# Gated linear attention plus a squared-ReLU MLP: later units' loads moved to GpSimd's queue, the K~ᵀv product one head pair behind, and three smaller moves

## The chip, the cores and the metric

The kernel runs on one core of a Trainium2 chip. The metric is the device time of one execution in microseconds (us); less is better. It was run three times for timing, and once more under the hardware profiler.

## The reference

A linear-attention recurrence with a complex decay runs over 768 steps for 4 batches and 8 heads of width 48. Its output, as 3072 rows of 384 numbers, goes through an MLP with a squared ReLU.

```python
mag = np.sqrt(a_re * a_re + a_im * a_im)
scale = np.minimum(mag, 0.999) / (mag + 1e-06)
a_re_n, a_im_n = (a_re * scale, a_im * scale)
for t in range(S):                      # S = 768
    ...
    S_re = ar * S_re - ai * S_im + kv   # kv = k_t outer v_t, per head
    S_im = ar * S_im + ai * S_re_old
    y[:, :, t] = einsum('bhd,bhde->bhe', q[:, :, t], S_re)
x = y.transpose(0, 2, 1, 3).reshape(3072, 384)
h = x @ w_in                            # 384 -> 2048
out = (np.maximum(h, 0) ** 2) @ w_out   # 2048 -> 384
```

## The kernel before

The work is cut into 8 **units**: a batch and one half (384 steps) of its sequence. A unit goes through four lists of small closures.

- **chain** (`chain_work`): `load` fetches a, q, k and v of the unit; VectorE (DVE) and ScalarE (ACT) normalise the decays (`roots`, `normalise`, `inverse`); `totals` turns totals per step group with TensorE (PE; tile `tot`) and `scan` multiplies them up on DVE; `back` turns them back (`bk`, copied to `xn`), and `apply` makes the decayed q and k (tile `QK`). The eight heads are two halves, z = 0 and z = 1: a, q, k, the `QK` tiles and the roots come in two parts. At its end `apply` writes k to a DRAM scratch (`rows<-QK`) and reads it back with time on the partitions (`KC<-rows`), both as DMAs of GpSimd's (POOL's) queue.
- **pair** (`pair_work`): for each of four head pairs, `turn` transposes q and k by step group c = 0, 1, 2 (PE `tq`, then ACT copies to `QKT`); `score` makes the causal scores (PE `sa`, DVE masks them into `A`); `keep` makes K~ᵀv (PE `kv`) and the running state (`St`, `S`); `mix` multiplies both out into `ypair`, ACT copies that to `yt`, and DMAs of SyncE's (SP's) queue put its rows into `xT`, the MLP's input.
- **hidden**: 16 blocks of 128 hidden columns (PE `h`, three matmuls each, one per 128 rows of `xT`); ACT squares into `g`. **project**: 3 row blocks in four parts of four matmuls (PE `o`), then `ot` to the output through SP's queue.

`merge` interleaves lists by relative position. In the steady part each merge holds hidden and project of unit n, pair of unit n+1 and chain of unit n+2. Before it come unit 0's chain; unit 0's pair list merged with the conversion of w_in; unit 1's chain and unit 0's hidden; unit 1's pair list merged with the conversion of w_out; unit 2's chain. The inputs are float64, and `convert` makes float32 of 32 weight pieces: one ACT instruction for the lower words (`more`), three on DVE. The merged program is then reordered within each engine by a scheduler with costs of its own, so the order in which an engine runs is not that of the code. Each engine works its own list in order.

Tiles that an engine waits for: `a` and `qk` have one buffer per half, so a load waits until `apply` of the unit before has written `QK`. The PSUM pools are `trp` (2 buffers, for `tq`, `kv`, `tot`, `bk`), `scp` (2, `sa`), `yp` (1, `ypair`) and `dp` (3, `h` and `o`).

Of the kernel before, what the change touches and what calls it, by code (L numbers as in the profile page):

```python
# [481 lines left out]
def fast_path(ctx, tc, q, k, v, a_re, a_im, moe_w_in, moe_w_out, out, flag):  # L482
# [26 lines left out]
    dve, pool, act = nc.vector, nc.gpsimd, nc.scalar  # L509
# [7 lines left out]
    wst = ctx.enter_context(tc.tile_pool(name="wst", bufs=4))  # L517
    trp = ctx.enter_context(tc.tile_pool(name="trp", bufs=2, space=PSUM))
# [3 lines left out]
    dp = ctx.enter_context(tc.tile_pool(name="dp", bufs=3, space=PSUM))  # L522
# [31 lines left out]
    wide = moe_w_in.dtype != F32  # L554
# [12 lines left out]
    raws = {}  # L567

    def fetch(i):
# [10 lines left out]
            out=raw.rearrange("p (m f) two -> p m (f two)", m=src.shape[1]), in_=src)  # L580
        after(get, mark["landed"])

    def convert(i):

        if wide:
            dst, _ = piece(i)
            raw = raws[i]
            lo, hi = raw[:, :, 0], raw[:, :, 1]
            bits = dst.bitcast(U32)

            more = wst.tile([C, DM], U32, name="more", tag="more", bufs=2)
            act.activation(out=more, in_=lo, func=AF.Copy, scale=2.0 ** -29)
# [7 lines left out]
            dve.tensor_tensor(out=bits, in0=bits, in1=more, op=ALU.add)  # L600
        n = i + (NF // 2 if i < NF else 4)
        if n < (NF if i < NF else 2 * NF):
            fetch(n)
# [19 lines left out]
    def load(u):  # L623
        def src(ap):
            return ap[u["b"], :, ts(u["half"], L), :]

        for name, pair in (("a", (a_re, a_im)), ("qk", (q, k))):
            for z in range(2):
                t = u[name, z] = nat.tile([C, 2, HH, W, D], F32, name=f"{name}{z}",
                                          tag=f"{name}{z}")  # L630
                for j, ap in enumerate(pair):
                    nc.sync.dma_start(
                        out=t[:, j].rearrange("p h c d -> p h (c d)"),
                        in_=src(ap)[ts(z, HH)].rearrange(LOADS, c=W))
        if u["n"] == 0:

            gate = const.tile([C, 2], F32, name="gate")
            pool.tensor_copy(out=gate[:, 0:1], in_=u["a", 0][:, 1, HH - 1, W - 1, D - 1:D])
            mark["landed"] = pool.tensor_copy(out=gate[:, 1:2],
                                              in_=u["a", 1][:, 1, HH - 1, W - 1, D - 1:D])  # L640
        u["v"] = pr.tile([C, NM, H, D], F32, name="v", tag="v")
        for j in range(W):
            nc.sync.dma_start(out=u["v"][:, j],
                              in_=src(v).rearrange("h (j s) d -> s j h d", s=C)[:, j])

    def flat(t):
        return t.rearrange("p h c d -> p (h c d)")
# [211 lines left out]
                            in_=rows.rearrange("(j p) e -> p j e", p=C)[:, 0:n])  # L859


    def turn(u, i, c):

        if c == 0:
            u.setdefault("T", {})[i] = pr.tile([R, 4, L], F32, name="QKT", tag="QKT")
        z = 2 * i // HH
        ps = trp.tile([R, 4, C], F32, name="tq", tag="tr")
        for j in range(2):
            for h in range(2):
                hh = (2 * i + h) % HH  # L870
                src = u["K", z][:, c, hh] if j else u["Q", z][:, hh, c]
                nc.tensor.transpose(ps[:, 2 * j + h], src, ident)  # L872
        act.copy(out=u["T"][i].rearrange("r z (p c) -> r c z p", c=W)[:, c], in_=ps)  # L873

    def score(u, i, h):

        T = u["T"][i]
        if h == 0:
            u.setdefault("A", {})[i] = pr.tile([C, 2, NM, C], F32, name="A", tag="A")
        sa = scp.tile([C, NM, C], F32, name="sa", tag="sc")  # L880
        for j in range(NM):
            nc.tensor.matmul(sa[:, j], lhsT=T[:, 2 + h, ts(j, C)], rhs=T[:, h, ts(j, C)],  # L882
                             start=True, stop=True)
        dve.tensor_tensor(out=u["A"][i][:, h], in0=sa, in1=mask3, op=ALU.mult)  # L884
# [3 lines left out]
    def keep(u, i):  # L888

        late = u["half"] > 0  # L890
        n = NM - u["half"]
        if i == 0 and not late:
            state[u["b"]] = wk.tile([R, H, D], F32, name="S", tag="S", bufs=2)
        total_s = state[u["b"]][:, 2 * i:2 * i + 2]
        ps = trp.tile([R, NM, 2, D], F32, name="kv", tag="tr")
        for j in range(n):
            for h in range(2):
                hh = 2 * i + h
                nc.tensor.matmul(ps[:, j, h], lhsT=u["KC", hh // HH][:, j, hh % HH],  # L899
                                 rhs=u["v"][:, j, hh], start=True, stop=True)  # L900
        st = pr.tile([R, 2, 2, D], F32, name="St", tag="St")
        u.setdefault("S", {})[i] = [total_s if late else None, st[:, 0], st[:, 1]]
        outs = [st[:, 0], st[:, 1], total_s]
        before = total_s if late else None
        for j in range(n):
            if before is None:
                act.copy(out=outs[j], in_=ps[:, j])
            else:
                dve.tensor_tensor(out=outs[j], in0=ps[:, j], in1=before, op=ALU.add)
            before = outs[j]  # L910
# [26 lines left out]
    def pair_work(u):  # L937
        w = []
        for i in range(NP):
            w += [[lambda i=i: turn(u, i, 0)], [lambda i=i: turn(u, i, 1)],  # L940
                  [lambda i=i: turn(u, i, 2)]]
# [163 lines left out]
```

## Time and profile before

| | us |
|---|---|
| median of 3 timed runs (841.29 to 846.20) | 844.82 |
| the profiled execution | 853.49 |
| its span, from first to last instruction | 851.8 |
| PE busy in the span (86%) | 728.8 |
| DVE busy (61%) | 519.6 |
| ACT busy (48%) | 407.5 |
| POOL busy (8%) | 65.5 |
| chain that ended last: PE's share | 46% |
| the same: DVE, DMA | 18%, 10% |

The page gives busy time by engine, the span in 40 slices with the granted PE clock, the chain of work that ended last, and the costliest groups of instructions with what their engine waited for. Times in the views are from the span's start. A float32 matmul is one row in the program's order and two halves in the trace. Unit 0's `QK` is ready at 56 us, unit 1's at 157, unit 2's at 247, unit 3's at 314; then a merge ends at 404, 497, 591 and 687, where the next unit's `QK` is ready and its pair list begins. I call those places **boundaries**.

### The profile page before, as it was taken

The page shows a single profiled execution, that of the slowest core. Times are in us where ns is not written, and L with a number is a line of the kernel's source. Part 1 is how long each engine was busy: PE and PEld are TensorE (multiplying, and loading weights), DVE is VectorE, ACT ScalarE, POOL GpSimd, SP SyncE. Part 2 cuts the span into 40 slices and gives each one's busy share as a digit, 9 for nine tenths or more (in the row PEclk, how much of TensorE's full clock was granted, in tenths as well). Part 3 has the DMA queues.
Part 4 walks back from the last instruction along what each step waited for, and adds up shares of the span by engine and source line. Part 5 has one row for each costly group of instructions (what it writes and reads, how often), then busy time and mean ns, then how long its engine had stood idle before and what let it go on. Part 6 is the DMA issues. An engine that isn't in the chain of part 4 may idle for free.

```text
span 851.8 us, 9873 instructions
## 1 busy us (share of the span) xinstructions
PE 728.8 (86%) x3474; PEld 471.4 (55%) x3474; DVE 519.6 (61%) x1316; ACT 407.5 (48%) x769; POOL 65.5 (8%) x107
## 2 busy tenths in 40 slices
PE   0138978499999989999699988999699989999995
PEld 0026644376556656666466655666466656666552
DVE  5895669978996985658472866378463856500000
ACT  5524377354657608931495237811693225411500
POOL 4003000120000000000000010000000034200000
PEclk9995779689999999999899998999899999999998
DMA  9337110662033026000800062002700178500000
GB/s 289 99 124 226 44 33 1 203 219 71 18 111 120 24 74 183 8 17 17 266 7 8 18 212 45 8 17 71 213 7 8 34 248 271 188 17 26 1 9 23
DMA packets 77114, 76.23 MB, mean 89 GB/s; under 512 B 29184, under 2 KB 68224, under 8 KB 77056
## 3 DMA queue, kind: packets, MB, share of 16 engines
q0 software_dynamic: 10496, 42.47, 14.8%
q1 hardware_dynamic: 66560, 33.04, 14.2%
q8 instruction: 29, 0.48, 0.2%
q14 instruction: 29, 0.24, 0.1%
HBM read 56.62 MB, written 14.16 MB: 83 GB/s over the span
## 4 chain that ended last, share of the span: by engine, by line
PE 46%; DVE 18%; DMA 10%; issue 3%; ACT 3%; SPq 1%; POOL 0%; POOLq 0%; ACTq 0%
PE h L953 20%; PE o L967 14%; DVE fa L786 5%; PE sa L882 3%; PE tq L872 3%; DMA a<-in_a_im_dram 3%; DMA xT<-yt 2%; PE ypair L918 2%; DMA look<-in_moe_w_in_dram 2%; PE kv L899 2%; PE ypair L923 2%; DMA look<-in_moe_w_out_dram 2%; DVE QK L849 1%; DMA KC<-rows 1%; DVE fb L789 1%
## 5 line engine op out<-in xcount | busy, mean ns | idle before, releaser
L953 PE MATMUL h<-xT,w 128*128 128x384 f32 x768 | 284.3, 510 | 27.1 <-DMA xT<-yt 23.9
L967 PE MATMUL o<-w,g 128*128 128x384 f32 x768 | 266.0, 492 | 0.0
L953 PEld LDWEIGHTS h<-xT,w 128*128 128x128 f32 x768 | 142.7, 199 | 110.3 <-issue 33.4
L967 PEld LDWEIGHTS o<-w,g 128*128 128x128 f32 x768 | 140.8, 192 | 83.5 <-issue 3.7
L873 ACT COPY QKT<-tq 96x512 f32<-96x512 f32 x96 | 80.8, 845 | 59.0 <-PE tq L872 58.8
L958 ACT ACTIVATE g<-h 128x384 f32<-128x384 f32 x128 | 62.0, 487 | 84.1 <-PE h L953 83.7
L872 PE MATMUL tq<-ident,QK 128*96 128x128 f32 x384 | 66.2, 304 | 24.9 <-DVE QK L849 14.5
L872 PEld LDWEIGHTS tq<-ident,QK 128*96 128x96 f32 x384 | 48.3, 141 | 55.3 <-issue 28.1
L959 ACT ACTIVATE g<-g 128x384 f32<-128x384 f32 x128 | 66.3, 523 | 2.4
L882 PEld LDWEIGHTS sa<-QKT 96*128 96x128 f32 x384 | 55.1, 207 | 17.0 <-ACT QKT L873 4.6
L882 PE MATMUL sa<-QKT 96*128 96x128 f32 x384 | 58.3, 295 | 2.6 <-ACT QKT L873 2.6
L884 DVE TENSOR_TENSOR A<-sa,mask 128x384 f32<-128x384 f32 x64 | 35.0, 553 | 41.4 <-PE sa L882 40.9
L971 ACT COPY ot<-o 128x384 f32<-128x384 f32 x24 | 11.4, 476 | 99.9 <-PE o L967 99.8
L786 DVE TENSOR_TENSOR fa<-e 128x192 f32<-128x192 f32 (+1 forms) x56 | 23.9, 455 | 55.7 <-ACT e L759 55.1
L856 POOL DMA_DIRECT2D rows<-QK x16 | 9.2, 574 | 479.5 <-DVE QK L849 312.6
L849 DVE TENSOR_TENSOR QK<-qk,a 128x576 f32<-128x576 f32 x64 | 44.6, 750 | 0.0
L899 PEld LDWEIGHTS kv<-v,KC 128*96 128x96 f32 x320 | 35.4, 183 | 12.8 <-issue 8.7
L918 PE MATMUL ypair<-A,v 128*48 128x128 f32 x384 | 42.1, 292 | 0.0
L1048 DVE TENSOR_SCALAR flag<-cnt 1x1 int32<-1x1 f32 x1 | 0.1, 145 | 68.4 <-PE cnt L1047 68.4
L899 PE MATMUL kv<-v,KC 128*96 128x48 f32 x320 | 35.2, 262 | 5.3 <-issue 2.7
L757 PE MATMUL tot<-ident,last 128*128 128x128 f32 x72 | 13.8, 295 | 28.8 <-ACT last L719 25.4
L657 ACT ACTIVATE fa<-a 128x1152 f32<-128x1152 f32 x16 | 18.6, 1160 | 39.5 <-DMA a<-in_a_im_dram 39.5
(104 smaller groups left out, 854.0 us busy)
## 6 DMA issues: line engine op xcount, KB each, us to landing
rows<-QK POOLq DMA_DIRECT2D x16, 576.0 KB, 4.7
raw<-in_moe_w_in_dram POOLq DMA_DIRECT2D x16, 384.0 KB, 6.5
raw<-in_moe_w_out_dram POOLq DMA_DIRECT2D x16, 384.0 KB, 4.4
look<-in_moe_w_in_dram POOLq DMA_DIRECT2D x16, 384.0 KB, 4.8
look<-in_moe_w_out_dram POOLq DMA_DIRECT2D x16, 384.0 KB, 4.2
a<-in_a_re_dram SPq DMA_DIRECT2D x16, 288.0 KB, 4.2
a<-in_a_im_dram SPq DMA_DIRECT2D x16, 288.0 KB, 4.9
qk<-in_q_dram SPq DMA_DIRECT2D x16, 288.0 KB, 5.4
```

The costliest lines, as they stand in the source:

```text
L786: dve.tensor_tensor(out=t, in0=x, in1=y[:, j].unsqueeze(1).to_broadcast(shape), op=ALU.mult)
L849: done = dve.tensor_tensor(out=o[:, :, :, r * D:(r + 1) * D], in0=qk[:, j], in1=a[:, r], op=ALU.mult)
L872: nc.tensor.transpose(ps[:, 2 * j + h], src, ident)
L873: act.copy(out=u["T"][i].rearrange("r z (p c) -> r c z p", c=W)[:, c], in_=ps)
L882: nc.tensor.matmul(sa[:, j], lhsT=T[:, 2 + h, ts(j, C)], rhs=T[:, h, ts(j, C)], start=True, stop=True)
L884: dve.tensor_tensor(out=u["A"][i][:, h], in0=sa, in1=mask3, op=ALU.mult)
L899: nc.tensor.matmul(ps[:, j, h], lhsT=u["KC", hh // HH][:, j, hh % HH], rhs=u["v"][:, j, hh], start=True, stop=True)
L918: nc.tensor.matmul(ypair[64 * h:64 * h + D, ts(j, C)], lhsT=u["v"][:, j, 2 * i + h], rhs=A[:, h, j], start=True, stop=S_j is None)
L953: nc.tensor.matmul(ps, lhsT=w1[:, f, m], rhs=u["xT"][:, m], start=(m == 0), stop=(m == NM - 1))
L958: act.activation(out=t, in_=ps, func=AF.Relu)
L959: act.activation(out=t, in_=t, func=AF.Square)
L967: nc.tensor.matmul(u["o"], lhsT=u["g"][f][:, ts(c, C)], rhs=w2[:, f], start=(f == 0), stop=(f == NF - 1))
```

## The change

- Loads of units 2 to 7 are issued by POOL's queue, not SP's. SP keeps the loads of units 0 and 1, the `xT` rows and the output.
- `keep(i)` follows pair i+1's turns and precedes its scores, and `mix(i)` stands between those two scores; three empty slots at the list's end bring the last `mix` forward.
- In units 0 and 1 the `tq` of group c = 1 and `kv` take their PSUM buffer from `dp`, not `trp`.
- The first state of a batch is copied from PSUM by DVE, not ACT.
- The lower words of a weight piece are taken by ACT one piece ahead.
- Two empty slots follow `load` in the chain list.

```diff
+    def lower(i):
+        if wide:
+            more = mores[i] = wst.tile([C, DM], U32, name="more", tag="more", bufs=2)
+            act.activation(out=more, in_=raws[i][:, :, 0], func=AF.Copy, scale=2.0 ** -29)
     def convert(i):
+        if i % NF == 0:
+            lower(i)
...
-            act.activation(out=more, in_=lo, func=AF.Copy, scale=2.0 ** -29)
...
+        if (i + 1) % NF:
+            lower(i + 1)
...
+        get = nc.sync if u["n"] < 2 else nc.gpsimd
...
-                    nc.sync.dma_start(
+                    get.dma_start(
                         out=t[:, j].rearrange("p h c d -> p h (c d)"),
...
-            nc.sync.dma_start(out=u["v"][:, j],
+            get.dma_start(out=u["v"][:, j],
...
+    def bank(u, shape, name, more):
+        pool, tag = (dp, "d") if more and u["n"] < 2 else (trp, "tr")
+        return pool.tile(shape, F32, name=name, tag=tag)
...
-        ps = trp.tile([R, 4, C], F32, name="tq", tag="tr")
+        ps = bank(u, [R, 4, C], "tq", c == 1)
...
-        ps = trp.tile([R, NM, 2, D], F32, name="kv", tag="tr")
+        ps = bank(u, [R, NM, 2, D], "kv", True)
...
-                act.copy(out=outs[j], in_=ps[:, j])
+                dve.tensor_copy(out=outs[j], in_=ps[:, j])
...
             if i:
-                w.append([lambda i=i: mix(u, i - 1)])
-            w += [[lambda i=i, h=h: score(u, i, h)] for h in range(2)]
-            w.append([lambda i=i: keep(u, i)])
-        w += [[], [lambda: mix(u, NP - 1)]]
+                w += [[lambda i=i: keep(u, i - 1)], [lambda i=i: score(u, i, 0)],
+                      [lambda i=i: mix(u, i - 1)], [lambda i=i: score(u, i, 1)]]
+            else:
+                w += [[lambda h=h: score(u, 0, h)] for h in range(2)]
+        w += [[lambda: keep(u, NP - 1)], [], [lambda: mix(u, NP - 1)], [], []]
...
-        return ([lambda: load(u)] + both(roots, normalise, inner, measure_roots, inverse)
+        return ([lambda: load(u), lambda: None, lambda: None] + both(roots, normalise, inner, measure_roots, inverse)
```

**The queues at the boundary at 404 us.** SP before: the eight loads of unit 5 (a, then q and k, for each half), an output store (`out_dram`), and the last two row transfers of unit 4 (`xT`) behind all of them.

```order
L973 DMA out_dram<-ot 128x384
L632 DMA a_2848<-in_a_re_dram 128x4x144
L632 DMA a_2848<-in_a_im_dram 128x4x144
L632 DMA qk_2854<-in_q_dram 128x4x144
L632 DMA qk_2854<-in_k_dram 128x4x144
L632 DMA a_2851<-in_a_re_dram 128x4x144
L632 DMA a_2851<-in_a_im_dram 128x4x144
L973 DMA out_dram<-ot 128x384
L632 DMA qk_2857<-in_q_dram 128x4x144
L632 DMA qk_2857<-in_k_dram 128x4x144
L934 DMA xT<-yt 48x384 x2
L643 DMA v<-in_v_dram 128x8x48 x3
```

POOL after, at the same place; before, only the two `rows` and then the two `KC` stood here.

```order
L866 DMA rows<-QK 128x1152
L642 DMA a_2848<-in_a_re_dram 128x4x144
L642 DMA a_2848<-in_a_im_dram 128x4x144
L642 DMA qk_2854<-in_q_dram 128x4x144
L868 DMA KC<-rows 128x3x384
L866 DMA rows<-QK 128x1152
L642 DMA a_2851<-in_a_re_dram 128x4x144
L642 DMA a_2851<-in_a_im_dram 128x4x144
L642 DMA qk_2854<-in_k_dram 128x4x144
L868 DMA KC<-rows 128x3x384
L642 DMA qk_2857<-in_q_dram 128x4x144
L642 DMA qk_2857<-in_k_dram 128x4x144
```

The loads have left SP's list; on POOL's, the second half's loads now stand behind the first `KC`, which waits until its `rows` have landed.

**PE and ACT at the same boundary.** PE before, from unit 3's last projections over unit 4's last `mix` (six `ypair` rows) to its first `h`:

```order
L967 MATMUL o<-w_109,g 128x384 x8
L918 MATMUL ypair<-A,v 48x128 x2
L923 MATMUL ypair<-QKT,S 48x128 x2
L918 MATMUL ypair<-A,v 48x128 x2
L923 MATMUL ypair<-QKT,St 48x128 x2
L918 MATMUL ypair<-A,v 48x128 x2
L923 MATMUL ypair<-QKT,St 48x128 x2
L872 MATMUL tq<-ident,QK 96x128 x4
L953 MATMUL h<-xT,w_108 128x384 x2
L872 MATMUL tq<-ident,QK 96x128 x4
L953 MATMUL h<-xT,w_108 128x384 x2
```

PE after:

```order
L933 MATMUL ypair<-A,v 48x128 x2
L938 MATMUL ypair<-QKT,S 48x128 x2
L933 MATMUL ypair<-A,v 48x128 x2
L938 MATMUL ypair<-QKT,St 48x128 x2
L933 MATMUL ypair<-A,v 48x128 x2
L938 MATMUL ypair<-QKT,St 48x128 x2
L982 MATMUL o<-w_109,g 128x384 x8
L887 MATMUL tq<-ident,QK 96x128 x4
L968 MATMUL h<-xT,w_108 128x384 x3
L887 MATMUL tq<-ident,QK 96x128 x4
L968 MATMUL h<-xT,w_108 128x384 x3
```

The eight `o` have moved between the last `mix` and the first `h`. ACT before, from the first half's `a` of unit 5 (its square, L657, the first of `roots`) to the first `QKT`:

```order
L657 ACTIVATE fa_2876,sums<-a_2848 128x1152
L971 COPY ot<-o 128x384
L662 ACTIVATE fa_2876<-fb_2877 128x576
L663 ACTIVATE fa_2876<-fa_2876 128x576
L926 COPY yt<-ypair 112x384
L873 COPY QKT<-tq 96x512
```

ACT after:

```order
L941 COPY yt<-ypair 112x384
L667 ACTIVATE fa_2906,sums<-a_2848 128x1152
L986 COPY ot<-o 128x384
L888 COPY QKT<-tq 96x512
L672 ACTIVATE fa_2906<-fb_2907 128x576
L673 ACTIVATE fa_2906<-fa_2906 128x576
```

The copy of the last `ypair` now stands ahead of the square that waits for the load, and not three instructions behind it.

**PE in unit 1's pair list.** Before, from its first `tq`:

```order
L872 MATMUL tq<-ident,QK 96x128 x12
L882 MATMUL sa<-QKT 128x128 x6
L899 MATMUL kv<-v,KC 96x48 x4
L872 MATMUL tq<-ident,QK 96x128 x12
L967 MATMUL o<-w_109,g 128x384 x2
```

After:

```order
L887 MATMUL tq<-ident,QK 96x128 x17
L897 MATMUL sa<-QKT 128x128 x6
L887 MATMUL tq<-ident,QK 96x128 x7
L914 MATMUL kv<-v,KC 96x48 x4
L887 MATMUL tq<-ident,QK 96x128 x12
L914 MATMUL kv<-v,KC 96x48 x4
```

The first `kv` stands behind two pairs' turns and not one's. The first `o` of unit 0 comes after all turns and all `kv` of the list, and 7 of them stand inside the list where 12 did.

More of the change, by code (lines that the diff above doesn't have):

```diff
@@ L581, in fetch @@
         after(get, mark["landed"])
+    mores = {}
+    def lower(i):
+        if wide:
+            more = mores[i] = wst.tile([C, DM], U32, name="more", tag="more", bufs=2)
+            act.activation(out=more, in_=raws[i][:, :, 0], func=AF.Copy, scale=2.0 ** -29)
     def convert(i):
+        if i % NF == 0:
+            lower(i)
         if wide:
             dst, _ = piece(i)
-            raw = raws[i]
-            lo, hi = raw[:, :, 0], raw[:, :, 1]
+            hi, more = raws[i][:, :, 1], mores[i]
             bits = dst.bitcast(U32)
-            more = wst.tile([C, DM], U32, name="more", tag="more", bufs=2)
-            act.activation(out=more, in_=lo, func=AF.Copy, scale=2.0 ** -29)
             first = dve.tensor_scalar(out=bits, in0=hi, scalar1=0x07FFFFFF, scalar2=3,
@@ L939, in pair_work @@
         for i in range(NP):
-            w += [[lambda i=i: turn(u, i, 0)], [lambda i=i: turn(u, i, 1)],
-                  [lambda i=i: turn(u, i, 2)]]
+            w += [[lambda i=i, c=c: turn(u, i, c)] for c in range(W)]
             if i:
-                w.append([lambda i=i: mix(u, i - 1)])
-            w += [[lambda i=i, h=h: score(u, i, h)] for h in range(2)]
-            w.append([lambda i=i: keep(u, i)])
-        w += [[], [lambda: mix(u, NP - 1)]]
+                w += [[lambda i=i: keep(u, i - 1)], [lambda i=i: score(u, i, 0)],
[3 more added lines that the diff above has]
+        w += [[lambda: keep(u, NP - 1)], [], [lambda: mix(u, NP - 1)], [], []]
         return [lambda fs=fs: [f() for f in fs] for fs in w]
```

2 lines of the change are left out of this document (1 added, 1 removed).

## The prediction

> **What bounds the kernel now.** I read the engines' busy shares first, then a table of stretches, then what PE waited for, then the time line at a boundary.
>
> ```profile
> PE 728.8 (86%) x3474; PEld 471.4 (55%) x3474; DVE 519.6 (61%) x1316; ACT 407.5 (48%) x769; POOL 65.5 (8%) x107
> ...
> 56.00:107.00 51.00, 42.34 (x236) 31.33 (x236) 33.96 (x77) 21.64 (x39) 8.36 (x11) 0.67 0.55 167
> 157.00:199.00 42.00, 37.92 (x249) 27.34 (x249) 33.43 (x80) 20.09 (x33) 9.02 (x15) 0.78 0.71 227
> ...
> 247.00:314.00 67.00, 62.65 (x335) 42.01 (x334) 55.77 (x141) 39.88 (x75) 2.75 (x5) 0.95 0.27 84
> 314.00:404.00 90.00, 87.92 (x445) 57.45 (x444) 60.68 (x154) 48.04 (x91) 2.47 (x4) 1.00 0.23 69
> 404.00:497.00 93.00, 85.93 (x438) 56.51 (x436) 55.77 (x140) 47.88 (x93) 2.65 (x4) 0.96 0.23 70
> ```
>
> The columns of a stretch are its length, then busy time (and count) of PE, weight loads, DVE, ACT, POOL, then the granted PE clock. From 247 us on PE is the bound, with 2 to 7 us idle in a merge. The two pair lists with conversions (56 to 107, 157 to 199) are different: PE is busy at a low clock, and DVE and ACT wait on it and it on them. What can still be taken is PE's idle time and its time at half clock. This is what it waited for:
>
> ```profile
> PE h L953 <- DMA xT<-yt: 23.9, 6, 6.1
> ...
> PE tq L872 <- ACT QKT L873: 9.3, 12, 1.6
> ...
> PE kv L899 <- issue: 2.7, 1, 2.7
> PE kv L899 <- DMA KC<-rows: 2.6, 2, 1.7
> ```
>
> The first row is the largest that the change touches: six waits for the last rows of `xT`. Four of them, at the boundaries at 404, 497, 591 and 687 us, stand here with the `tq` just ahead, and the boundary at 404 in full:
>
> ```profile
> 403.23 5.39 PE L967 MATMUL o<-w,g 128*128 128x384 f32 x16
> 403.75 0.40 SPq L632 DMA_DIRECT2D a<-in_a_re_dram  x1
> 409.69 0.39 PE L923 MATMUL ypair<-QKT,St 96*48 96x128 f32 x4
> 409.83 1.16 ACT L657 ACTIVATE fa<-a 128x1152 f32<-128x1152 f32 x1 [9.14 <-DMA a<-in_a_im_dram]
> 413.22 0.46 ACT L926 COPY yt<-ypair 112x384 f32<-112x384 f32 x1
> 413.70 1.19 SPq L934 DMA_DIRECT2D xT<-yt  x2
> 414.46 0.64 PE L872 MATMUL tq<-ident,QK 128*96 128x128 f32 x4 [0.79 <-ACT QKT L873]
> 421.75 4.24 PE L953 MATMUL h<-xT,w 128*128 128x384 f32 x8 [6.00 <-DMA xT<-yt]
> 426.50 2.10 PE L953 MATMUL h<-xT,w 128*128 128x384 f32 x6
> 508.75 0.64 PE L872 MATMUL tq<-ident,QK 128*96 128x128 f32 x4 [1.58 <-ACT QKT L873]
> 514.33 5.46 PE L953 MATMUL h<-xT,w 128*128 128x384 f32 x8 [4.29 <-DMA xT<-yt]
> 601.77 0.64 PE L872 MATMUL tq<-ident,QK 128*96 128x128 f32 x4 [0.56 <-ACT QKT L873]
> 609.12 4.42 PE L953 MATMUL h<-xT,w 128*128 128x384 f32 x8 [6.06 <-DMA xT<-yt]
> 698.27 2.90 PE L953 MATMUL h<-xT,w 128*128 128x384 f32 x4 [3.40 <-DMA xT<-yt]
> ```
>
> `mix` ends at 410.1, yet its rows are there only at 421.75. ACT spends 3.1 us first on the square that waited for the load and on three more instructions; then copy and issue take 1.7; then the transfer, behind eight loads in one queue, takes 6.9 (414.89 to 421.75). PE pays twice, since the matmuls behind a wait are slow: 8 halves take 4.24, 5.46 and 4.42 us and four take 2.90, where the row at 426.50 gives 0.35 for one.
>
> **The change part by part.**
>
> *Rows alone on SP, `mix` earlier, roots two slots later: the boundaries.* The waits are 6.00 + 4.29 + 6.06 + 3.40 = 19.75; the three `tq` waits 2.93; the slow matmuls (4.24 - 2.8) + (5.46 - 2.8) + (4.42 - 2.8) + (2.90 - 1.4) = 7.2. Together 29.9 us are at stake. In the changed order the copy stands ahead of the square, so the 3.1 goes, and between the last `ypair` and the first matmul on the late rows stand 16 halves of `o` (5.4), a `tq` (0.6) and four halves of `h` (1.4): 7.4 us. In them the copy (0.5), the issue (1.2) and the transfer must fit. The rows for the transfer are the quiet median and the boundary at 687, where SP carried no loads but POOL's queue was full of weight reads:
>
> ```profile
> xT<-yt SPq DMA_DIRECT2D x48, 72.0 KB, 2.2
> ...
> 691.82 1.16 SPq L934 DMA_DIRECT2D xT<-yt  x2
> ```
>
> There it took 698.27 - 692.98 = 5.3 us. So the sum is 3.9 to 7.0 against 7.4, and I take 5.3, the nearer case: no wait for the rows. What is late next is ACT: the square waits for `a` with `QKT` copies queued behind it, and PE's third `tq` and first `sa` wait for those. I put 1.2 us on each of the four boundaries, the size of the `tq` waits above: 29.9 - 4.8 = 25.
>
> The Trainium skill (DMA: Bandwidth & Descriptors, "Issuing engines are not separate DMA queues") says that transfers started from SP, ACT or POOL run on the same 16 engines, and that starting them from several saves only issue time. By that, the transfer stays at 6.9 us; it is a rival below. The same page ("Queues, rings and completion order") says that each engine takes packets in turn from the queues it has work for, by which rows need not wait out all the loads; 5.3 with POOL full against 6.9 in one queue leans that way, but is one pair of places.
>
> *Loads on POOL: their own cost.* 11 DMAs per unit, 66 in all, move. POOL's price is bounded by these:
>
> ```profile
> L858 POOL DMA_DIRECT2D KC<-rows x16 | 12.0, 752 | 48.4 <-PE tq L872 14.5 <-DMA rows<-QK 13.3 <-PE o L967 9.0
> L856 POOL DMA_DIRECT2D rows<-QK x16 | 9.2, 574 | 479.5 <-DVE QK L849 312.6 <-DVE St L909 160.8 <-DVE S L909 6.0
> ```
>
> `rows` has 128 runs and `KC` up to 384, so 256 more runs cost about 0.2 us; a load has 512 runs (v 1024): 0.85 and 1.25 us if linear, and 2.3 and 4.6 if in proportion to `rows`. I take the line through both rows: 8 x 0.85 + 3 x 1.25 = 11 us a unit on an engine busy 2.65 us in a merge of 93: nothing. The second half's `a` now stands behind `KC`'s wait for its `rows`, some 4 us, and one more `rows`, so it is issued at about 411 where SP issued it at 407; `KC` too comes a few us later, but its reader, `kv`, has moved back a pair. The chain has cover for that:
>
> ```profile
> 447.39 0.34 ACT L720 COPY last<-fb 128x192 f32<-128x192 f32 x1
> ...
> 457.89 0.49 PE L757 MATMUL tot<-ident,last 128*128 128x128 f32 x3
> ```
>
> `last` is complete 10 us ahead of the first `tot`. PE will arrive about 7 us sooner, but in the new order `tot` stands one `h` and one `mix` (3.4 us) further back, so some 6 us are left: nothing lost.
>
> *The pair lists with conversions.* `keep` one pair behind, `dp` buffers and lower words ahead all act here. DVE and PE waited, in 56 to 107:
>
> ```profile
> DVE w L600 <- ACT more L592: 16.0, 8, 3.4
> ...
> PE tq L872 <- ACT QKT L873: 4.0, 5, 0.9
> PE kv L899 <- issue: 2.7, 1, 2.7
> PE sa L882 <- ACT QKT L873: 0.9, 1, 0.9
> ...
> 106.66 0.69 ACT L662 ACTIVATE fa<-fb 128x576 f32<-128x576 f32 x1
> ```
>
> The next unit's chain goes on at 106.66, when PE's last `mix` is copied, and from there to 156 it is bound by DVE and ACT. So what PE saves is saved: 7.6 us of waits, of which I leave 1 for `KC`. DVE has its 34 us of work from 56 on and isn't in the way once `more` is early. In 157 to 199 PE's waits of this kind are 2.0 + 0.9 + 0.9 = 3.8, but another thing moves: the `o` that stood among the pair work go behind it. Of the stretches, this is the share of `h` in the first and `o` in the second (PE's column):
>
> ```profile
> 56.00:107.00 51.00, 6.19 (x12) 2.29 (x12) 0.67 0.55 167
> ...
> 157.00:199.00 42.00, 10.96 (x25) 4.56 (x25) 0.78 0.71 227
> ...
> 160.00:170.00 10.00, 6.64 (x30) 5.20 (x28) 8.26 (x18) 3.54 (x5) 3.15 (x5) 0.50 1.01 331
> 170.00:180.00 10.00, 9.70 (x60) 6.99 (x60) 4.89 (x12) 5.28 (x11) 1.91 (x3) 0.73 0.61 200
> 180.00:190.00 10.00, 9.85 (x86) 7.43 (x86) 9.23 (x25) 6.49 (x13) 3.41 (x6) 1.00 0.81 247
> ```
>
> The same kind of pair work took 42.3 - 6.2 = 36 us at a clock of 0.67 and 37.9 - 11.0 = 27 at 0.78; in the second stretch the clock rose to 1.00 after `o` came in at 171. Without them it may stay at half: up to 9 us more. With fewer pauses it may also rise early in both: up to 9 us less in the first stretch, where DVE's 34 us end at about 90. I take half of the loss in the second (-4.6 + 3.8, about -1) and no rise in the first: 6.6 - 1, so 6 us, between ends of 1 and 20. Of the waits of 3.1 and 2.3 us for the scan in 200 to 314 I change nothing.
>
> *The copy by DVE.* 16 instructions of 0.25 us move to an engine that next waits for the same `kv` anyway: nothing.
>
> The sum is 25 + 6 = 31 us on the execution of 853.49 (span 851.8), so 822. That execution is 8.7 us above the timed median of 844.82. Where those 8.7 are no view shows; if they are in the boundaries' transfers, which is where time varies with other traffic, the gain there is smaller by as much. I take half of that, 4: 844.8 - 27 = 817.8, say 817.
>
> **The rivals.** *The queues share all*: the transfer stays at 6.9, and 0.5 + 1.2 + 6.9 = 8.6 against 7.4 leaves 1.2 us of wait at each boundary, which brings back the slow matmuls, 1.8 each: 4 x 3.0 = 12 us, so 829. For it speaks 3.40 us of wait at 687 with SP's queue free of loads; against it, that ACT and PE's order alone give most of the gain.
>
> *The clock stays low in unit 1's list and nothing comes of unit 0's*: the early 6 us become 0 or -3: 823 to 826. For it speaks 0.50 while PE was nearly full from 71 to 80 us with small matmuls.
>
> *The clock rises early*: 10 us more, so 807 and below. For it speaks that the list now starts with 17 `tq` in a row. The skill's page TensorE: Matmul & The Clock Gate ("What's actually happening") has the clock set by how busy PE has lately been, in windows of about 3.4 us; by that, closed pauses would be enough for this rival, and the stretch at 71 to 80 doesn't bear it out.
>
> *Slower, through POOL's queue*: all loads need POOL's time, and the square that waits for `a` stands ahead of three `QKT`. Each us that two loads take longer than 0.85 each delays PE once ACT's 2 us of slack are gone. At 5 us a load, 2 x 4.1 - 2 = 6.3 at each of five boundaries, 31 us, eats the gain; from there on it is slower (at 6 us, 855). Against it speaks that 384 runs took 0.75.
>
> *The waits move on*: PE comes 7 us earlier to `tot` and `bk`, and the chain isn't ready. If the 6 us of slack are 3 short at four merges, 12 us return: 829, or no change with the early part lost too.
>
> **How the numbers follow.** The forecast (808 to 823) has a chance of 0.46; shared queues (about 829) 0.17; nothing early (823 to 826) 0.14; early clock (798 to 808) 0.12; waits that move on 0.07, a third of it within 0.5%; slower 0.04. The range goes from 799, the early clock without the 4 us taken off, to 835, shared queues with nothing early, and leaves out about 0.15. A difference under 0.5%, 4 us, can't be told from no change here. That gives 0.92 faster, 0.04 the same, 0.04 slower.
>
> **What would show it.** In the changed profile: no wait of `h` for `xT` over 2 us at the four boundaries, and a granted clock of 1.00 there; loads as POOL rows under 1 us (v under 1.4); merges of about 85 to 87 us from 404 to 591 in place of 93 and 94; DVE's wait for `more` under 5 us in unit 0's list and the next chain at about 100. Wrong would be: waits for `xT` of 3 us or more; `tq` or `sa` waiting over 3 us for `QKT` behind a late square; `tot` waiting for `last`; unit 1's list at half clock to its end.

## The result, and the profile after

The changed kernel takes 818.22 us (median of 4 runs, 817.69 to 822.13), the kernel before 845.51 beside it (4 runs, 841.29 to 848.36). The ratio is 0.969, with a 95% interval of 0.964 to 0.974: 27 us faster, where 817 was forecast. The profiled execution after has a span of 815.9 us, 36 shorter than the one before; the two medians differ by 27. What is read below from single profiled executions adds up to the 36 and not to the 27.

The busy times, and what PE waited for:

```profile
PE 712.4 (87%) x3474; PEld 462.8 (57%) x3474; DVE 519.6 (64%) x1332; ACT 399.7 (49%) x753; POOL 116.4 (14%) x173
```

```profile
PE sa L897 <- ACT QKT L888: 8.0, 6, 2.0
...
PE h L968 <- DMA xT<-yt: 3.2, 2, 2.4
```

The waits of `h` for `xT` have gone from 23.9 to 3.2 us, and what is left lies in unit 0's part. The wait of `sa` for `QKT` has grown from 2.6 to 8.0, while that of `tq` for it has fallen from 9.3 to 1.6. The stretches, with the same columns as in the prediction (PE, weight loads, DVE, ACT, POOL, PE's clock): first unit 0's pair list, then three merges and what follows the last.

```profile
56.00:98.00 42.00, 34.49 (x230) 26.95 (x230) 33.73 (x81) 19.50 (x33) 9.97 (x13) 0.80 0.63 199
...
392.40:480.00 87.60, 86.30 (x444) 56.84 (x441) 57.76 (x148) 47.10 (x91) 12.06 (x16) 1.00 0.24 75
480.00:564.40 84.40, 83.07 (x432) 54.70 (x430) 55.09 (x144) 46.13 (x89) 10.41 (x16) 1.00 0.23 73
564.40:652.80 88.40, 86.55 (x438) 57.01 (x434) 57.24 (x150) 47.17 (x90) 12.72 (x18) 0.98 0.25 79
652.80:815.90 163.10, 151.49 (x630) 94.32 (x626) 40.90 (x93) 47.33 (x88) 22.04 (x34) 0.98 0.31 101
```

Before, the three merges took 93.4, 94.2 and 94.9 us at a clock of 0.96, and the rest from 686.5 to 851.8 took 165.3. The four gains are 5.8, 9.9, 6.5 and 2.2: 24.4 us for the four boundaries. Another 8.5 come ahead of unit 1's `QK`, read off the rows in which POOL first writes its `rows`, before and after; the 3 that are left lie between there and unit 4's `QK`.

```profile
156.01 0.57 POOL L856 DMA_DIRECT2D rows<-QK  x1 [70.35 <-DVE QK L849]
```

```profile
147.47 0.57 POOL L866 DMA_DIRECT2D rows<-QK  x1 [48.51 <-DVE QK L859]
```

The boundary that stood at 404 us before, on the time line after:

```profile
392.29 0.39 PE L938 MATMUL ypair<-QKT,St 96*48 96x128 f32 x4
392.61 5.43 PE L982 MATMUL o<-w,g 128*128 128x384 f32 x16
392.77 0.48 ACT L941 COPY yt<-ypair 112x384 f32<-112x384 f32 x1 [3.61 <-PE ypair L938]
393.27 1.24 SPq L949 DMA_DIRECT2D xT<-yt  x2
393.35 0.75 POOL L642 DMA_DIRECT2D a<-in_a_re_dram  x1 [0.35 <-ACT yt L941]
...
398.31 2.10 PE L968 MATMUL h<-xT,w 128*128 128x384 f32 x6
399.10 1.16 ACT L667 ACTIVATE fa<-a 128x1152 f32<-128x1152 f32 x1 [5.85 <-DMA a<-in_a_im_dram]
...
406.46 0.94 PE L897 MATMUL sa<-QKT 96*128 96x128 f32 x6 [1.30 <-ACT QKT L888]
```

The copy to `yt` follows the last `ypair` at once, its rows are issued half a microsecond later, and 16 halves of `o` cover the transfer. PE waits only for `sa`, 1.30 us, behind the square that waited for its load. The issues' time to landing (last column) at this boundary, before and then after:

```profile
xT<-yt SPq DMA_DIRECT2D x2, 72.0 KB, 7.5
```

```profile
xT<-yt SPq DMA_DIRECT2D x2, 72.0 KB, 4.0
```

### The profile page after: what moved, and what is told of

It reads as the page before. It is cut to its first block, busy times and chain, and to the rows that moved or that the text cites. A ratio compares the mean times of both kernels' runs of the same rounds, so it can differ in the third digit from the quotient of the medians.

```text
span 815.9 us, 9921 instructions
## 1 busy us (share of the span) xinstructions
PE 712.4 (87%) x3474; PEld 462.8 (57%) x3474; DVE 519.6 (64%) x1332; ACT 399.7 (49%) x753; POOL 116.4 (14%) x173
## 2 busy tenths in 40 slices
DMA packets 38043, 76.24 MB, mean 93 GB/s; under 512 B 10752, under 2 KB 25216, under 8 KB 37984
## 4 chain that ended last, share of the span: by engine, by line
PE 49%; issue 18%; DVE 14%; DMA 9%; ACT 6%; SPq 2%; POOL 1%; ACTq 0%; POOLq 0%
PE o L982 19%; PE h L968 17%; PE sa L897 4%; DMA a<-in_a_im_dram 3%; DVE fa L796 3%; PE tq L887 2%; PE ypair L933 2%; DMA look<-in_moe_w_in_dram 2%; PE ypair L938 2%; PE kv L914 2%; DVE QK L859 2%; ACT QKT L888 2%; DMA v<-in_v_dram 2%; DMA rows<-QK 1%; SPq L653 1%
## 5 line engine op out<-in xcount | busy, mean ns | idle before, releaser
L968 PE MATMUL h<-xT,w 128*128 128x384 f32 x768 | 273.1, 497 | 6.9 <-ACT g L973 3.6
L968 PEld LDWEIGHTS h<-xT,w 128*128 128x128 f32 x768 | 140.0, 193 | 87.0 <-issue 9.3
L887 PE MATMUL tq<-ident,QK 128*96 128x128 f32 x384 | 60.5, 291 | 16.9 <-DVE QK L859 15.2
L941 ACT COPY yt<-ypair 112x384 f32<-112x384 f32 x32 | 15.2, 476 | 93.3 <-PE ypair L938 93.3
L914 PEld LDWEIGHTS kv<-v,KC 128*96 128x96 f32 x320 | 32.6, 172 | 13.9 <-DMA KC<-rows 3.9
L914 PE MATMUL kv<-v,KC 128*96 128x48 f32 x320 | 33.5, 253 | 5.8 <-DMA KC<-rows 3.6
```

Of the source, the lines that this page charges most:

```text
L968: nc.tensor.matmul(ps, lhsT=w1[:, f, m], rhs=u["xT"][:, m], start=(m == 0), stop=(m == NM - 1))
```

## The experiments

In the table, "order" is the new list of pair work with its three empty slots, "bank" the `dp` buffers for `tq` and `kv`. The last two columns are from one profiled execution of each: when unit 1's first `rows` are written, and the time from unit 4's first `rows` to the end, in which all four boundaries lie.

| kernel | median, us (range) | ratio to before (95%) | unit 1's `rows` | unit 4's to end |
|---|---|---|---|---|
| before, second profile | 848.58 (one run) | | 153.4 | 449.6 |
| after, again | 820.28 (812.54 to 825.78) | 0.9705 (0.9645 to 0.9766) | 143.5 | 423.1 |
| before + loads on POOL | 831.65 (823.95 to 837.82) | 0.9871 (0.9816 to 0.9926) | 149.4 | 429.2 |
| before + order and slots | 819.12 (814.51 to 822.74) | 0.9694 (0.9651 to 0.9737) | 142.1 | 438.7 |
| after, loads on SP | 829.21 (827.83 to 838.77) | 0.9859 (0.9802 to 0.9916) | 144.5 | 434.8 |
| after, last `mix` last | 837.92 (833.58 to 846.70) | 0.9929 (0.9893 to 0.9965) | 143.0 | 442.9 |
| before + bank, lower words, DVE copy | 849.45 (842.28 to 850.77) | 1.0039 (1.0002 to 1.0075) | 147.4 | 447.8 |
| after, without bank and lower words | 810.16 (802.17 to 816.59) | 0.9594 (0.9533 to 0.9655) | 139.7 | 421.7 |
| after, bank for `kv` alone | 821.14 (816.94 to 825.94) | 0.9698 (0.9651 to 0.9745) | 151.0 | 424.2 |
| the one without bank and lower words, ACT copy | 804.24 (798.39 to 808.29) | 0.9501 (0.9458 to 0.9545) | 139.0 | 420.4 |
| the same with DVE copy, without slots | 807.96 (803.91 to 815.79) | 0.9542 (0.9489 to 0.9596) | 139.9 | 422.6 |
| after, loads split in four | 814.21 (809.72 to 817.94) | 0.9610 (0.9568 to 0.9652) | 146.7 | 422.8 |

The profiled execution before was 447.8 from unit 4's `rows` on; after, 423.5.

### Only the loads move

```diff
-                    nc.sync.dma_start(
+                    get.dma_start(        # get = nc.sync if u["n"] < 2 else nc.gpsimd
```

> Only the loads of units 2 to 7 move to POOL's queue; the order of pair work, buffers, copies and lower words stay as before. In the profiles of before and after, the last rows of xT took 7.5, 5.8, 7.5 and 5.9 us from issue to landing at the boundaries, and 4.0, 3.9, 3.9 and 2.9 afterwards. Theory A (queue and order both needed; the queue shortens the transfer, the order hides what is left): transfers of about 4 us, so each of the first three waits of h for xT falls by some 2 to 3.5 us, but about 2.5 us of wait and the slow matmuls behind it remain at each boundary: 8 to 12 us gained, 833 to 837 us. Rival B (order alone decides; the queue is worth nothing): 842 to 848, waits as before. Rival C (the queue alone decides): 820 to 826, no wait over 1 us.

12 us faster. The time line at the boundary near 404, the same place's transfer, and the stretches behind three of the four waits (0.79, 1.00 and 1.00 is PE's clock):

```profile
399.14 0.48 ACT L927 COPY yt<-ypair 112x384 f32<-112x384 f32 x1 [0.94 <-PE ypair L924]
399.65 1.16 SPq L935 DMA_DIRECT2D xT<-yt  x2
...
405.32 2.05 PE L954 MATMUL h<-xT,w 128*128 128x384 f32 x4 [2.63 <-DMA xT<-yt]
```

```profile
xT<-yt SPq DMA_DIRECT2D x2, 72.0 KB, 4.7
```

```profile
404.00:412.00 8.00, 6.68 (x22) 4.27 (x23) 1.52 (x2) 5.98 (x12) 3.96 (x5) 0.79 1.04 305
490.00:498.00 8.00, 6.85 (x27) 3.79 (x26) 0.76 (x1) 5.82 (x11) 7.82 (x10) 1.00 0.96 317
580.00:588.00 8.00, 6.30 (x25) 3.92 (x26) 1.98 (x4) 6.49 (x12) 3.91 (x5) 1.00 1.04 306
```

The time is 1.4 us below theory A's range, and the waits are of its kind: the transfer takes 4.7 in place of 7.5, and a wait is left. In the profiled execution, the fastest of the six, 18.6 us are gone from unit 4's `rows` to the end, more than the 8 to 12 expected. The rows show two reasons: the copy is no longer late here (the reordering put it ahead of the square), and behind three of the four waits the clock stayed at 1.00.

That the queue itself shortens the transfer is not shown by this. When these rows were issued, only two of unit 5's eight loads of a, q and k had been issued (at 393.60 and 397.45 us); before, all eight stood ahead of them (403.75 to 412.37). The next run has a say in this.

### The last mix last again

```diff
-        w += [[lambda: keep(u, NP - 1)], [], [lambda: mix(u, NP - 1)], [], []]
+        w += [[lambda: keep(u, NP - 1)], [], [lambda: mix(u, NP - 1)]]
```

> The changed kernel without the two empty slots behind the last mix, so that the last mix comes last again: no o stands between it and the first h of the unit, only one tq and two h; loads stay on POOL's queue. Copy 0.5, issue 1.2 and a transfer of 4.0 make 5.7 us against 0.6 + 0.7 + 0.6 + 0.7 = 2.6 us of work. Theory A: a wait of 2 to 4 us for xT at each of the four boundaries and slow matmuls of 1.8 behind it, 15 to 23 us lost, 833 to 841. Rival B (order decides through the copy's place ahead of the square alone, not through the cover): 816 to 822. Rival C (queue decides): 816 to 822 with waits under 1 us.

Theory A, inside its range: 838. Two empty slots are worth 2.3% here, though the loads stay on POOL's queue. The copy comes among the first `h`, behind the square again and so 1.5 us after the last `ypair`, and PE runs out of work:

```profile
399.53 0.46 ACT L941 COPY yt<-ypair 112x384 f32<-112x384 f32 x1
...
400.01 1.19 SPq L949 DMA_DIRECT2D xT<-yt  x2
...
406.67 1.62 PE L968 MATMUL h<-xT,w 128*128 128x384 f32 x2 [4.78 <-DMA xT<-yt]
```

The transfer took 5.9 us here, not 4.0. Six of the eight loads had been issued ahead of it (392.98 to 399.86 us), in the changed kernel none (the first at 393.35, behind the rows' own issue at 393.27). So the run moves three things together: the work that covers the transfer, the copy's place behind the square, and the loads ahead of the rows.

At the first three boundaries the transfer took 5.9, 5.8 and 6.1 us with the loads on POOL's queue, against 7.5, 5.8 and 7.5 before, with the loads on SP's. With much started ahead of the rows it is long on either queue. What part of the remaining 1 us, on the mean, is the queue's, no run separates.

### Only the order, and the changed kernel with loads on SP

```diff
# the first: before, with pair_work and the two slots behind load as changed
# the second, against after:
-        get = nc.sync if u["n"] < 2 else nc.gpsimd
+        get = nc.sync
```

> Before with the new order of pair work (keep a pair behind, mix between the scores, three empty slots at the end) and the two empty slots after load; loads on SP, buffers, state copy and lower words as before. Theory A: as the kernel with loads on SP, less the early part (about 6 to 8 us): 830 to 838. Rival B (order alone gives the boundaries' 25 us): 820 to 825, no wait of h for xT over 1 us at the four boundaries, and unit 0's list as long as before (56 to 107). Rival C: 840 to 848.

> The changed kernel with all loads back on SP's queue; all else as changed. The last rows of xT now stand ahead of all but one of the next loads in SP's list, because the copy of the last ypair is earlier. Theory A (both needed): the transfer shares SP's queue again and takes 5.8 to 7.5 us, with copy 0.5 and issue 1.2 that is 7.5 to 9.2 against 7.4 us of cover: waits of 0 to 1.8 us and slow matmuls of 1.8 us at three or four boundaries, 824 to 832. Rival B (order alone decides): 816 to 821, no wait of h for xT over 1 us. Rival C (queue alone decides): waits of 4 to 6 us as before, 838 to 844.

The order alone gives 819, as fast as the whole change; the second kernel 829. In neither does `h` wait over 1.6 us for `xT`. The second kernel's transfer:

```profile
xT<-yt SPq DMA_DIRECT2D x2, 72.0 KB, 3.8
```

So 3.8 us with the loads on the same queue: once the copy is early, the rows stand ahead of the loads in SP's list, and for this transfer it no longer matters whose list the loads are in. On this, rival B was right and theory A wrong. But the order-only kernel comes to B's time by another way than B's: at the boundaries the order gave 9 us (447.8 to 438.7), not 25, since a new wait took the place of the old. Of the other 22 us by which its profile is shorter, 14 lie ahead of unit 1's `rows` and 8 between these and unit 4's. In the order-only kernel:

```profile
388.08 0.37 SPq L632 DMA_DIRECT2D a<-in_a_re_dram  x1
...
389.35 0.60 SPq L632 DMA_DIRECT2D a<-in_a_im_dram  x1
...
397.36 1.16 ACT L657 ACTIVATE fa<-a 128x1152 f32<-128x1152 f32 x1 [3.36 <-DMA a<-in_a_im_dram]
...
398.89 0.83 ACT L873 COPY QKT<-tq 96x512 f32<-96x512 f32 x1
```

The second half's load is issued at 389.35, its data come 8 us later, the square waits for it on ACT, and a copy that PE's `sa` needs stands behind the square: `sa` waits 4.84 us. That is the "square waits for `a` with `QKT` copies queued behind it" of the prediction, at four times its size. The kernel with queue and order, but without the rest (804.24 us in the table), at the same place:

```profile
383.20 0.75 POOL L634 DMA_DIRECT2D a<-in_a_im_dram  x1
...
389.53 0.83 ACT L880 COPY QKT<-tq 96x512 f32<-96x512 f32 x1
...
390.29 1.16 ACT L659 ACTIVATE fa<-a 128x1152 f32<-128x1152 f32 x1
390.41 0.94 PE L889 MATMUL sa<-QKT 96*128 96x128 f32 x6 [1.39 <-ACT QKT L880]
```

Here the copy stands ahead of the square and the square finds its data: 1.39 us. What the queue buys once the order is in place, 15 us from 819.12 to 804.24, is therefore in the loads and in ACT's list, not in the rows.

### The early parts

```diff
# one kernel: before + lower(), bank(), and
+                dve.tensor_copy(out=outs[j], in_=ps[:, j])
# the other: after, with more made in its own piece, and
-        ps = bank(u, [R, 4, C], "tq", c == 1)
+        ps = trp.tile([R, 4, C], F32, name="tq", tag="tr")
...
-        ps = bank(u, [R, NM, 2, D], "kv", True)
+        ps = trp.tile([R, NM, 2, D], F32, name="kv", tag="tr")
```

> Before with the lower words a piece ahead, the dp buffers in units 0 and 1, and the first state copied by DVE; queue, order and slots as before. Theory A: 836 to 840, unit 0's list 6 us shorter, boundaries as before with waits for xT of 3 to 6 us. Rival D: 841 to 847, DVE's wait for more gone from unit 0's list but unit 1's QK no earlier than in the second profile of the kernel before.

> The changed kernel with the lower words taken in their own piece and with all tq and kv in the two trp buffers, as before; queue, order of pair work, slots and DVE copy as changed. Theory A (these parts give some 6 us in unit 0's and unit 1's lists): 822 to 826, unit 1's QK 4 to 8 us later than in the changed kernel of this call, PE waiting again for QKT and DVE for more in unit 0's list. Rival D (the list's length is set by the clock and by DVE's work, not by these waits; nothing is gained): 815 to 820, unit 1's QK at 142 to 149.

Both go against theory A. Alone the early parts give nothing (849), and taken out of the changed kernel they make it 10 us faster, which rival D had not expected either. The order-only kernel (819) and the changed one with loads on SP (829), which differ in the early parts alone, are 10 us apart too. The lower words a piece ahead are easily told: with them or without, once the buffers are the same, the scheduler builds the same program, the same instructions in the same order on every engine, waits included, so that edit does nothing. All of the 10 us belong to the buffers. DVE's wait for `more` in unit 0's list (56 to 107) was 16.0 us before; after, and in the kernel without the early parts:

```profile
DVE w L606 <- ACT more L589: 5.0, 2, 3.6
```

```profile
DVE w L600 <- ACT more L592: 0.6, 1, 0.6
```

With the new order this wait is 0.6 to 2.9 us in the four kernels without the buffers, and 2.0 to 8.9 in the profiles with them.

One profile of unit 0's list does not tell what an edit there is worth. In the kernel where only later loads move, PE, ACT and DVE run this list in the same order as before, and yet its last copy of `ypair` comes at 98.3 us, before at 106.3, and DVE waits 8.1 us for `more`, before 16.0. What differs is the clock, which rose 20 us earlier; PE's clock is the third number from the end, first before, then with the loads moved:

```profile
80.00:86.00 6.00, 5.46 (x28) 3.68 (x30) 4.43 (x11) 3.07 (x6) 2.33 (x3) 0.50 0.44 131
```

```profile
80.00:86.00 6.00, 5.07 (x50) 4.13 (x51) 5.24 (x13) 3.32 (x7) 1.52 (x2) 1.00 0.74 209
```

All the profiles together tell more. Unit 1's `rows` come at 147 to 156 us in the four without the order, at 143 to 151 in the six with order and buffers, and at 139 to 142 in the four with the order and no such buffers. So the early parts' 147.4 alone, 6.0 and 8.6 us ahead of the two profiles before, is no gain that can be told from the 149.4 of the kernel that has none of them.

One more run asked which of the two buffers does it:

```diff
-        ps = bank(u, [R, 4, C], "tq", c == 1)
+        ps = trp.tile([R, 4, C], F32, name="tq", tag="tr")
```

> The changed kernel with kv alone in the dp buffers in units 0 and 1 and every tq in trp; all else as changed. The kernel with both back in trp took 810, the changed one 818 to 820. Theory E (tq in dp does the harm: PE then runs 17 tq and 7 more ahead of the first kv, and ACT's QKT copies of them stand ahead of the lower words that DVE waits for): 807 to 813. Rival F (kv in dp does the harm): 817 to 822. If both do: 812 to 817.

Rival F: `kv` in `dp` is enough for the loss. On PE's time line, this kernel:

```profile
75.02 3.11 PE L914 MATMUL kv<-v,KC 128*96 128x48 f32 x18 [4.70 <-DMA KC<-rows]
```

and the changed kernel, with its next copies of `ypair`:

```profile
75.88 1.16 PE L914 MATMUL kv<-v,KC 128*96 128x48 f32 x6 [2.21 <-ACT more L589]
...
84.56 0.48 ACT L941 COPY yt<-ypair 112x384 f32<-112x384 f32 x1 [7.53 <-PE ypair L938]
```

and without the early parts:

```profile
77.10 0.48 ACT L933 COPY yt<-ypair 112x384 f32<-112x384 f32 x1 [1.46 <-PE ypair L930]
```

With buffers to spare, the scheduler puts `kv` further ahead in PE's list, in front of `sa` and `ypair` of the pair before. In these executions PE waits there with those queued behind it, in the first kernel for `KC`; in the changed one the row names `more`, which `kv` doesn't read, so what it waited for is not told by it. The second `ypair` is 7.5 us later (84.56 against 77.10), and the clock falls too: from 74 to 80 us it is 0.51 in the changed kernel and 1.00 without the early parts.

```profile
74.00:80.00 6.00, 4.12 (x19) 3.12 (x20) 4.24 (x13) 1.97 (x4) 2.23 (x3) 0.51 1.04 325
```

```profile
74.00:80.00 6.00, 5.25 (x50) 3.96 (x49) 5.72 (x16) 3.91 (x7) 1.29 (x2) 1.00 1.02 327
```

The changed kernel's second profile, in the same order, has no wait at this `kv`, its second copy at 80.2 and a clock of 1.00 in that stretch. So that `kv` in `dp` costs the 10 us is shown by the times; that it costs them by this wait is shown in the first kernel alone. Over 74 to 98 us the clock was 0.58 to 0.88 in the six profiles with order and buffers and 0.90 to 1.00 in the four without these buffers. Nor does all of the loss lie in this list: 4 us of it stand between unit 3's and unit 4's `rows` (88.9 against 84.8), where no unit uses these buffers but the order on ACT and POOL has changed with them.

### The copy's engine, the two slots, and POOL's price

```diff
# on the kernel without the early parts
-                dve.tensor_copy(out=outs[j], in_=ps[:, j])
+                act.copy(out=outs[j], in_=ps[:, j])
```

> The kernel with tq and kv back in trp and the lower words in their own piece (810 us), with the first state copied by ACT as before. Theory A (the copy's engine is worth nothing): 807 to 813. Rival H (16 copies of 0.25 us on ACT, ahead of QKT in its list and behind kv, hold PE at the boundaries as in the kernel with the order alone, where sa waited 4.8 us): 815 to 822.

804.24, below theory A's range by 3 and against rival H: the copy on ACT is no slower, and by the ratios (0.9501 and 0.9594, whose intervals just overlap) rather some 1% faster. No row of the two profiles carries the difference (spans 796.7 and 800.3), so its cause stays open. This kernel, before plus queue, order and slots alone, is the fastest of all: 5.0% below the kernel before, and its interval ends below that of the changed one.

```diff
# on the kernel without the early parts
-        return ([lambda: load(u), lambda: None, lambda: None] + both(roots, ...
+        return ([lambda: load(u)] + both(roots, ...
```

> The same kernel (810 us) without the two empty slots behind load, so that the roots come two places earlier in the list. Theory A (the slots keep the square that waits for a out of the way of QKT): sa waits 2 to 4 us at four boundaries and PE is slow behind it, 815 to 824. Rival I (the reordering within ACT places the square either way; the slots are worth nothing): 807 to 813.

807.96 against 810.16: rival I, the slots are worth nothing that can be told.

```diff
# on the changed kernel, units 2 to 7
-                    get.dma_start(out=t[:, j]...
+                    for s in range(HH):   # one head each
+                        get.dma_start(out=t[:, j, s:s + 1]...
```

> The changed kernel with each load of a, q and k of units 2 to 7 split by head into four DMAs of 128 runs on POOL's queue: 32 in place of 8 a unit. At 0.55 to 0.75 us each a load costs POOL 2.2 to 3.0 us in place of 0.75. Theory A (as the prediction priced POOL: each us beyond 2 us of slack that two loads take longer delays PE by one at each boundary): 2 x 1.45 to 2 x 2.25 less 2 is 0.9 to 2.5 at five boundaries, 822 to 832, sa waiting 2 to 4 us for QKT. Rival G (POOL's time is hidden, since QKT copies can go ahead of the square): 815 to 821.

814.21, a little below rival G's range: nothing is lost. The row of POOL, and PE's wait at `sa`:

```profile
L644 POOL DMA_DIRECT2D a<-in_a_re_dram x48 | 25.7, 540 | 4.8 <-ACT QKT L890 1.6 <-DVE QK L861 1.1 <-ACT g L976 1.0
```

```profile
PE sa L899 <- ACT QKT L890: 1.1, 3, 0.5
```

A load's four parts cost POOL 2.2 us in place of 0.75, and `sa` waits less than before the split, not more. Rival G was right, and its reason too: the first of ACT's `QKT` copies now go ahead of the square.

### Both kernels once more

> The kernel before, profiled once more. Its first profiled execution was 8.7 us above the timed median, and unit 1's QK came at 156.0 us; a kernel that differs only in the loads of later units had it at 149.4. Theory D (the 8.7 us lie in unit 0's pair list, whose clock differs from one execution to the next): an execution near the median has unit 1's QK at 146 to 150 and the four merges from 314 on at 372 us in sum as before. Theory A' (they lie in the boundaries' transfers, as the prediction guessed): unit 1's QK at 155 to 157 again and the four merges together 4 to 8 us shorter.

> The changed kernel, profiled and timed once more, to set its spread beside the others. 816 to 821; the four merges from unit 3's QK on 347 to 352 us in sum; unit 1's QK anywhere from 142 to 149.

The second execution before was 848.58, 4.9 us shorter than the first. From unit 4's `rows` on it was 449.6 against 447.8, so nothing of the 4.9 lies at the boundaries; by then it was already 6.9 ahead (397.2 against 404.0), of which 2.6 came before unit 1's `rows` and the rest spread up to unit 4's. Neither D nor A' is met: unit 0's list ended as before. After, the second profile had 423.1 and 423.5 in that part, and 143.5 against 147.5 at unit 1's `rows`. The boundaries repeat within 2 us; the early part varies by 3 to 4 here, and by 8 in the list compared above.

## Why the prediction was right, step by step

**Boundaries, 25 us: right in size, half right in cause.** 24.4 in the first pair of profiles, 26.5 in the second (449.6 to 423.1). The budget held: copy, issue and a transfer of 4.2, counted from the end of the issue (5.3 was taken), fit into 7.4 us of PE's work, and the clock stayed at 1.00 but for two short stretches. The charge of 1.2 us each for `sa` behind the late square measured 1.30 to 1.85 in three of them. What failed is the sentence that gives the gain to "rows alone on SP": in the changed order the rows are ahead of the loads on either queue, 3.8 us against 4.0. What the queue gave at the boundaries (11 us, 434.8 to 423.5, between the kernels with the loads on SP and on POOL) is the shorter wait of `sa` behind the late square, to which the prediction gave 1.2 us a boundary.

Nor is the reading of the 5.3 us at 687 as a sign for taking turns borne out. With the loads alone moved, the transfer went from 7.5 to 4.7, but with two loads ahead of it in place of eight; with six ahead on POOL's queue it took 5.9. By the Trainium skill (DMA: Bandwidth & Descriptors, "Issuing engines are not separate DMA queues") moving them saves issue time only, and these rows do not speak against it. The same page of the Trainium skill ("Queues, rings and completion order") has engines take packets in turn from their queues; no run separates this from how much was started ahead, or from the packets, of which the whole program has 77114 with the loads on SP's queue and 38043 with them on POOL's.

**POOL's price: right.** A load took 0.75 us (0.85 forecast) and `v` 0.89 (1.25):

```profile
L653 POOL DMA_DIRECT2D v<-in_v_dram x18 | 15.9, 890 | 97.4 <-issue 70.5 <-PE ypair L933 19.2 <-PE ypair L938 7.6
L642 POOL DMA_DIRECT2D a<-in_a_re_dram x12 | 9.1, 760 | 7.0 <-DVE QK L859 4.1 <-DVE w L600 1.0 <-ACT g L974 1.0
```

The parts of the split loads, 128 runs each, took 0.54, so the line through few and many runs was the right bound. That the chain has cover for a later load held too: `tot` waits in no merge.

**Early lists, +6: size near, cause wrong.** 8.5 and 9.9 us were gained ahead of unit 1's `rows` in the two pairs of profiles. The prediction gave them to order, buffers and lower words together. The order gives them (139 to 142 in the four profiles with it and without the buffers); the buffers cost some 10 us of the total and the lower words are no change. The step that failed is the reading of the waits in unit 0's list, DVE's 16 us for `more` above all, as a fixed cost that buffers and an earlier place of `more` in the code would remove: in the same order it was 8.1 us in an execution whose clock rose sooner, and with the new order alone 2.9. For unit 1's list the forecast of about nothing held (91.3 and 91.7 from its `rows` to unit 2's).

**DVE's copy, nothing:** some 1% lost, at the edge of what can be told. **Half of the 8.7 us of the profiled execution in the boundaries, -4:** not borne out; the second profile has the same boundaries and is shorter ahead of them. The terms read from the profiles, 24.4 + 8.5 + 3, make the 36 us between two profiled executions and not the 27 between the medians; which of them is smaller in a median execution is not known. The -4 has nothing measured to stand for it, and the buffers' loss wasn't forecast. So it is partly luck that a sum of 27 met a measured 27.

**The rivals.** Shared queues (829): not what happened, though the kernel with loads on SP came to 829 by the other wait. Waits that move on to `tot`: none. Slower through POOL: fell with the split loads, whose 1.4 us more each should have cost PE 2 x 1.4 - 2 = 0.8 us at a boundary, 4 in all, and cost none. The early clock (807 and below) comes nearest in the kernels with queue and order and without the `dp` buffers: 0.94 to 1.00 from 74 to 98 us, and 804, 808 and 810.

## What to carry to other kernels

When a transfer is late, look first at what stands ahead of it on the engine that copies and in the queue that issues, and at how much work the reader has in between: here two empty slots at a list's end (2.3%) did as much as a queue of its own (1.3% alone, 2.0% on top of the order). How long the transfer takes went with what had been started ahead of it. Removing a wait sends the load behind it to the next consumer on the same engine, so read that engine's list too; and a spare buffer is not free where a scheduler uses it to move an instruction ahead of its data. Take a bundle of edits apart before keeping it: of these six, queue and order did the work, the lower words and the two slots behind `load` did nothing that can be told, and the buffers cost 1 to 2%. And compare medians before reading a stretch off two profiles: one and the same list took 8 us more or less by its clock alone.

## What the hardware showed that was not expected

A wait of PE can cost clock as well as its own time, and its length alone does not tell whether it will. Behind waits of 0.7, 3.0 and 2.5 us at three boundaries of the loads-only kernel the granted clock stayed at 1.00. Behind one of 2.63 it had a short stretch at 0.5 (0.79 in the first row of that kernel). Behind one of 1.82 in the changed kernel's second profile it was at 0.50 from 489.2 to 492.5 us, and six halves of `h` took 3.66 us in place of 2.10:

```profile
488.48 1.11 PE L897 MATMUL sa<-QKT 96*128 96x128 f32 x6 [1.82 <-ACT QKT L888]
489.38 3.66 PE L968 MATMUL h<-xT,w 128*128 128x384 f32 x6
```

Behind 4.8 to 5.4 us it fell to 0.68 to 0.79 over the next 8 us (the kernel with the last `mix` last), and behind 6.0 us to half (before, 418 to 424 us):

```profile
405.00:413.00 8.00, 6.33 (x20) 3.95 (x21) 0.64 (x1) 4.41 (x9) 4.67 (x6) 0.79 0.84 235
```

```profile
418.00:424.00 6.00, 2.25 (x4) 1.37 (x5) 3.43 (x4) 3.50 (x6) 0.00 (x0) 0.50 0.88 197
```

At these boundaries the clock was at half for about 3.4 us (406.2 to 409.6 in the loads-only kernel) or 6.8 us (417.8 to 424.6 before) at a time. The Trainium skill (TensorE: Matmul & The Clock Gate, "What's actually happening") has the clock set by windows of about 3.4 us that run freely, and these lengths agree with it. That a wait's place in such a window decides what it costs would fit, but no run here tests it.
